# Queries of a half spaced apart, gathered rows in an old score tile, and four raw weight buffers, in a fused attention and mixture-of-experts kernel

## The chip, the cores and the metric

The kernel runs on one core of one Trainium2 chip. The metric is the device time of one execution in microseconds. Four engines do the work beside the DMAs: TensorE (PE, with its weight loads PEld), VectorE (DVE), ScalarE (ACT) and GpSimd (POOL); SyncE (SP) issues most DMAs.

## The reference

```python
# q, k, v: [8, 12, 448, 64]; w_pre, w_post: [12, 12]
scores = (1 / 8) * np.matmul(q, k.transpose(0, 1, 3, 2))
scores = np.einsum('bhij,hg->bgij', scores, w_pre)      # mixed over heads
attn = np.exp(scores - scores.max(-1, keepdims=True))
attn = attn / (attn.sum(-1, keepdims=True) + 1e-09)
attn = np.einsum('bhij,hg->bgij', attn, w_post)         # mixed again
x = np.matmul(attn, v).transpose(0, 2, 1, 3).reshape(3584, 768)

logits = x @ w_gate                                     # 8 experts, the best one each
expert_idx = np.argmax(logits, axis=1)
gate_w = softmax(logits)[arange, expert_idx]
for e in range(8):
    xe = x[expert_idx == e]
    out[expert_idx == e] = gate_w[...] * (np.maximum(xe @ w1[e], 0) @ w2[e])
# w1: [8, 768, 1024]; w2: [8, 1024, 768]; all float32
```

## The kernel before

**Attention.** A batch has four tiles of queries: three of 120 and one of 88, 32 tiles `T` in all. A tile is worked in blocks `s` of 20 queries (`NB`), a block in two halves `c` of 10 (`IB`); `geom` holds for each tile its batch, its number of queries and the sizes of the halves by block. A tile of 120 has six blocks, one of 88 five, the last with one half of 8. The steps of a tile:

- `qk` (L191 to L205): the scores of 6 pairs of heads, three matmuls per head (high and low parts of float32), copied from PSUM into the score tile `si` by ACT (L204) and DVE (L205). In `si` a partition is a query and holds 12 heads × 448 keys.
- `relayout` (L211 to L217): for each half one DMA on SP (L216) from `si` to `sb`, so that a partition of `sb` is a pair of query and head, 120 of them behind the first four. The four `sb` tiles are used in turn.
- `mix` (L219): one matmul per half with the 124 × 124 matrix `Wpre` (L226), which mixes the heads of each of ten queries; DVE takes the row maxima (L227), ACT the exponentials and their sums (L228).
- `weigh` (L233): reciprocals on DVE, and on POOL the second mixing matrix scaled by them, `wp` (L241).
- `post` (L245): four matmuls per half (L252), whose result is the mixed attention with the keys on partitions, then a copy of each half from PSUM into `PT` (L258), half 0 by ACT, half 1 by DVE. `PT` holds for each chunk of keys and each head the queries of the tile in order.
- `av` (L262): attention times `v` for the whole tile; `rows` (L278): its transposition, the store of the rows to DRAM (`XD`, L292) and the logits; `choose` (L298) and `dispatch` (L319): the expert of each query, its place in the expert's list, and a scatter of row number and gate weight into the table `TB`.

**The order of attention** is written out by hand (loop at L476). Step `u` of the loop issues the relayout of block u+2, the mix of u, the post of u−2, the weights of u, and then what is entered in `after` for that block: at the third block of a tile `values` (av) of the tile before and `scores` of the tile after, which makes that block long on PE (a burst); `rows` at the fourth and fifth; the load of the queries of T+2 (two DMAs on SP, L104) one block before the last; loads and splits of keys and values of the next batch. The last six steps load w1 of expert 0 (`load_w`): `fill_w` fetches 128 rows of raw weights on SP into a tile of the pool `wrp` (`raw`, L404), ACT casts the high part (L405), DVE subtracts for the low part (L406).

**The experts** (loop at L593) have a capacity of 512 rows each; further rows would be handled in a loop at the end. The first 256 rows of expert 0 are gathered and turned (transposed) while attention ends, into the old score tile of pool `si_p[0]` (`first_gather`, `first_turn`). For the rest `load_x` (L516) reads the expert's list (L518), makes row numbers of it on DVE (`ti` L521, `tcl` L522) and gathers the rows by indirect DMAs on POOL (L525) into `xs`; `turn_x` transposes them (L541); `hidden` computes relu(x·w1) (L558) and fills w2 on the way; `result` computes the output (L578), weighs it and scatters it (L587). The last slot of 128 rows of an expert is computed only when it has more than 384 rows. The order of instructions of this part is set by the framework's scheduler, which takes buffers as constraints.

Of the kernel before, what the change touches and what calls it, by code (L numbers as in the profile page):

```python
# [8 lines left out]
F32 = mybir.dt.float32  # L9
F32R = mybir.dt.float32r  # L10
# [26 lines left out]
ROWS = NE * NT  # L37
# [5 lines left out]
def attn_moe_kernel(ctx, tc, qT, kT, v, w_pre, w_post, w_gate, w1, w2, out):  # L43
    nc = tc.nc
# [4 lines left out]
    XD = dram.tile([NT, HD], F32, name="XD")  # L49
    TB = dram.tile([ROWS, 2], F32, name="TB")  # L50

    geom = []
    for T in range(NTILE):
        it = T % 4
        ni = min(IT, S - it * IT)
        geom.append((T // 4, it, ni, [[min(IB, ni - i) for i in range(s, min(s + NB, ni), IB)]
                                      for s in range(0, ni, NB)]))


    kq = ctx.enter_context(ExitStack())  # L60
# [1 line left out]
    q_p = kq.enter_context(tc.tile_pool(name="qp", bufs=1, side="right"))  # L62
# [5 lines left out]
    si_p.append(att.enter_context(tc.tile_pool(name="sip1", bufs=1)))  # L68
    sb_p = att.enter_context(tc.tile_pool(name="sbp", bufs=1))
    e_p = att.enter_context(tc.tile_pool(name="ep", bufs=4))  # L70
    sm_p = att.enter_context(tc.tile_pool(name="smp", bufs=4))
    pt_p = att.enter_context(tc.tile_pool(name="ptp", bufs=2))
    x_p = att.enter_context(tc.tile_pool(name="xp", bufs=1))
    ps_s = att.enter_context(tc.tile_pool(name="ps_s", bufs=1, space=PSUM))
# [22 lines left out]
        KK[b, c] = (kh, kl)  # L97

    def load_q(T):
        b, it, ni, _ = geom[T]  # L100
        qr = q_p.tile([P, NPAIR, IT], F32, name="qr")
        src = qT[b, :, H * it * IT:H * (it * IT + ni)].rearrange("d (c t i) -> t d c i", c=NPAIR, t=2)
        for half in range(2):
            nc.sync.dma_start(out=qr[half * D:(half + 1) * D, :, :ni], in_=src[half])  # L104
        QR[T] = qr
# [74 lines left out]
                   allow_small_or_imprecise_dtypes=True)  # L180


    none = sm_p.tile([P, ROWS // P // 8, 2], F32, name="none", bufs=1)
    nc.gpsimd.memset(none, 0.0)
    nc.gpsimd.iota(none[:, :, 0].bitcast(I32), pattern=[[0, ROWS // P // 8]], base=NOROW,
                   channel_multiplier=0)
# [2 lines left out]


    def qk(T, c):  # L191
        b, it, ni, _ = geom[T]
        if c == 0:
            SI[T] = si_p[T % 2].tile([IT, H, S], F32, name="si")
        kh, kl = KK[b, c]
        qh, ql = QQ[T]

        bs = bank_s[c % 2]
        for n, (qx, kx) in enumerate(((qh, kh), (qh, kl), (ql, kh))):
            for r in range(2):  # L200
                hs = slice(r * D, (r + 1) * D)
                nc.tensor.matmul(out=bs[:ni, r, :S], lhsT=qx[hs, c, :ni], rhs=kx[hs, :],  # L202
                                 start=(n == 0), stop=(n == 2))
        nc.scalar.copy(out=SI[T][:ni, 2 * c, :], in_=bs[:ni, 0, :S])  # L204
        nc.vector.tensor_copy(out=SI[T][:ni, 2 * c + 1, :], in_=bs[:ni, 1, :S])  # L205
# [5 lines left out]
    def relayout(T, s):  # L211
        sb = sbs[nsb["n"] % len(sbs)]
        nsb["n"] += 1
        for c, nq in enumerate(geom[T][3][s]):
            q0 = s * NB + c * IB
            nc.sync.dma_start(out=sb[R0:R0 + nq * H, c, :], in_=SI[T][q0:q0 + nq])  # L216
# [28 lines left out]
    def post(T, s):  # L245
        if s == 0:
            PT[T] = pt_p.tile([JC, NJ, H, IT], F32, name="pt")
        et, wp = EE.pop((T, s))
        for n, nq in enumerate(geom[T][3][s]):
            pp = bank_p[n]  # L250
            for c in range(NJ):
                nc.tensor.matmul(out=pp[:, c * IT:(c + 1) * IT],  # L252
                                 lhsT=et[:R1, n, c * JC:(c + 1) * JC],
                                 rhs=wp[:R1, n, :], start=True, stop=True)
        for n, nq in enumerate(geom[T][3][s]):
            i0 = s * NB + n * IB
            copy = (nc.scalar.copy, nc.vector.tensor_copy)[n]
            copy(out=PT[T][:, :, :, i0:i0 + nq].rearrange("p c h i -> p (c h) i"),  # L258
                 in_=bank_p[n][:, :NJ * IT].rearrange("p (x i) -> p x i", i=IB)[:, :, :nq])


    def av(T, g):  # L262
        b, it, ni, _ = geom[T]
        if g == 0:
            XT[T] = x_p.tile([P, NPAIR, IT], F32, name="xt")
        pa = bank_s[g][:, 0, :3 * IT].rearrange("p (c i) -> p c i", i=IT)
        for p in range(3):
            for c in range(NJ):
                for r in range(2):
                    h = 2 * (3 * g + p) + r  # L270
                    nc.tensor.matmul(out=pa[r * D:(r + 1) * D, p, :ni],  # L271
                                     lhsT=VV[b][:, c, h * D:(h + 1) * D],
                                     rhs=PT[T][:, c, h, :ni], start=(c == 0), stop=(c == NJ - 1))
        nc.vector.tensor_copy(out=XT[T][:, 3 * g:3 * g + 3, :ni], in_=pa[:, :, :ni])
# [201 lines left out]
    for u in range(NU + PLAG):  # L476
        if u + RLEAD < NU:
            relayout(*blocks[u + RLEAD])
        if u < NU:
            mix(*blocks[u])  # L480
        if u >= PLAG:
            post(*blocks[u - PLAG])
        if u < NU:
            weigh(*blocks[u])
            for what in after.get(blocks[u], []):
                what[0](*what[1:])
            T, s = blocks[u]
# [28 lines left out]
    def load_x(e, s0=0):  # L516
# [3 lines left out]
        tc_ = xs_p.tile([P, NS], I32, name="tcl", bufs=3)  # L520
        nc.vector.tensor_copy(out=ti, in_=tb[:, :, 0].bitcast(I32))  # L521
        nc.vector.tensor_scalar(out=tc_, in0=ti, scalar1=NT - 1, scalar2=None, op0=ALU.min)  # L522
        xs = xs_p.tile([P, NS, HD], F32, name="xs")
        for s in range(s0, NS):
            nc.gpsimd.indirect_dma_start(  # L525
                out=xs[:, s, :], out_offset=None, in_=XD[:, :],
                in_offset=bass.IndirectOffsetOnAxis(ap=tc_[:, s:s + 1], axis=0),
                bounds_check=NT - 1, oob_is_err=False)
        XS[e] = (xs, tb, ti)

    def turn_x(e, sl):
        xs = XS[e][0]
        if e not in XX:
            XX[e] = (xt_p.tile([P, NK1, CAP], F32R, name="xh"),
                     xt_p.tile([P, NK1, CAP], F32R, name="xl"))
        for half in range(2):
# [1 line left out]
            xh, xl = (t[:, ks, sl * P:(sl + 1) * P] for t in XX[e])  # L538
            px = pm_x.tile([P, 512], F32, name="pm_x")[:, :3 * P].rearrange("p (k x) -> p k x", x=P)
            for k in range(3):  # L540
                nc.tensor.transpose(out=px[:, k, :], in_=xs[:, sl, (3 * half + k) * P:  # L541
                                                            (3 * half + k + 1) * P], identity=ident)
            nc.scalar.copy(out=xh, in_=px)  # L543
            nc.vector.tensor_sub(out=xl, in0=px, in1=xh.bitcast(F32))
# [220 lines left out]
```

## Time and profile before

| what | value |
|---|---|
| time before, median of 3 runs | 1835.14 us (1822.03 to 1836.98) |
| the profiled execution's own time | 1846.31 us |
| its span | 1844.5 us, 30106 instructions |
| mean granted TensorE clock | 0.948 |
| DMA | 197.55 MB, mean 107 GB/s |
| attention | about 40 to 1205 us |
| experts | about 1230 to 1845 us |

The profile is of one execution. Engines are named PE, PEld, DVE, ACT and POOL; a `q` behind a name is the queue that issues (SPq). A group is written `line engine operation out<-in xcount`. Where an instruction starts late, the bracket behind it gives the idle time of its engine ahead of it and what ended that time. The granted clock is the share of full speed that TensorE was allowed to run at.

### The profile page before, as it was taken

What the parts mean: (1) busy time and instruction counts of PE and PEld (TensorE: products, weight loads), DVE (VectorE), ACT (ScalarE), POOL (GpSimd) and SP (SyncE); (2) the same over time, 40 slices, a digit from 0 to 9 for tenths busy, and PEclk for the clock granted to TensorE, in tenths of its full rate; (3) what the DMA queues carried; (4) which work ended last, traced back from release to release, by engine and by line L of the source; (5) the groups of instructions that cost most, each with busy time, mean ns of one, the idle gap of its engine ahead of it and who ended that gap; (6) DMA issues with size and microseconds to landing.
All of it is one profiled execution on the core that took longest, in us unless ns stands there. A gap on an engine that the chain in (4) does not pass through costs nothing. (4 is left out here: it accounts for less than half of the span.)

```text
span 1844.5 us, 30106 instructions
## 1 busy us (share of the span) xinstructions
PE 1572.8 (85%) x11200; PEld 1263.9 (69%) x11200; DVE 812.0 (44%) x2023; ACT 705.1 (38%) x1616; POOL 428.0 (23%) x595
## 2 busy tenths in 40 slices
PE   3798898788888798888789789769999898998996
PEld 1566566566566566666566567569887887897986
DVE  1455455555455455455455545541433324333330
ACT  2344445444444345344445444431423223223230
POOL 4223223223224124223322322210110101101000
PEclk9999899999999899899899989976999999999998
DMA  3554554454455355345455444541523325244230
GB/s 91 124 110 88 103 132 81 105 132 91 86 130 116 73 125 121 79 111 123 80 123 107 89 90 91 124 127 43 171 100 128 127 79 173 97 136 151 86 109 32
DMA packets 114741, 197.55 MB, mean 107 GB/s; under 512 B 40018, under 2 KB 89186, under 8 KB 114580
## 3 DMA queue, kind: packets, MB, share of 16 engines
q1 hardware_dynamic: 107472, 171.51, 39.2%
q0 software_dynamic: 6064, 23.86, 3.4%
q8 instruction: 101, 1.65, 0.4%
q14 instruction: 60, 0.49, 0.1%
q10 hardware_dynamic: 1044, 0.04, 0.0%
HBM read 96.02 MB, written 23.06 MB: 65 GB/s over the span
## 5 line engine op out<-in xcount | busy, mean ns | idle before, releaser
L226 PE MATMUL bm<-sb,Wpre 124*124 124x448 f32 x720 | 349.4, 594 | 151.8 <-DMA sb<-si 120.7
L252 PEld LDWEIGHTS bp<-wp,et 124*112 124x112 f32 x2880 | 346.0, 188 | 84.0 <-issue 81.9
L241 POOL TENSOR_SCALAR wp<-Wpost,st 124x120 f32<-124x120 f32 x360 | 206.2, 584 | 828.6 <-DVE st L238 725.8
L228 ACT ACTIVATE et<-bm,st 124x448 f32<-124x448 f32 x360 | 226.5, 632 | 328.9 <-DVE st L227 328.9
L252 PE MATMUL bp<-wp,et 124*112 124x120 f32 x2880 | 347.9, 277 | 5.0 <-ACT pt L258 5.0
L226 PEld LDWEIGHTS bm<-sb,Wpre 124*124 124x124 f32 x720 | 120.8, 196 | 267.0 <-issue 135.0
L227 DVE TENSOR_REDUCE st<-bm 124x1 f32<-124x448 f32 x360 | 218.3, 620 | 174.1 <-PE bm L226 163.4
L204 ACT COPY si<-bs 120x448 f32<-120x448 f32 (+1 forms) x192 | 102.1, 532 | 254.8 <-PE bs L202 248.1
L258 DVE COPY pt<-bp 112x480 f32<-112x480 f32 x176 | 115.6, 657 | 155.2 <-PE bp L252 139.2
L558 PE MATMUL pm_h<-xh,al 128*128 128x512 f32 (+2 forms) x384 | 153.7, 400 | 13.3 <-DVE al L406 13.3
L205 DVE COPY si<-bs 120x448 f32<-120x448 f32 (+1 forms) x192 | 119.3, 624 | 102.4 <-ACT si L204 91.5
L271 PE MATMUL bs<-pt,vt 112*64 112x120 f32 (+1 forms) x3072 | 157.7, 264 | 0.6 <-ACT pt L258 0.6
L558 PE MATMUL pm_h<-xh,ah 128*128 128x512 f32 (+2 forms) x384 | 152.3, 397 | 5.3 <-DVE hl L562 3.0
L271 PEld LDWEIGHTS bs<-pt,vt 112*64 112x64 f32 x3072 | 150.9, 140 | 4.7 <-ACT pt L258 0.9
L558 PE MATMUL pm_h<-xl,ah 128*128 128x512 f32 (+2 forms) x384 | 152.1, 396 | 0.0
L587 POOL DMA_INDIRECT out<-y,ti x30 | 34.3, 1142 | 499.1 <-ACT xh L543 327.4
L202 PE MATMUL bs<-kh,qh 64*120 64x448 f32 (+1 forms) x384 | 86.9, 449 | 50.3 <-DVE si L205 37.5
L578 PE MATMUL pm_y<-bh,hh 128*128 128x384 f32 x480 | 129.6, 348 | 0.0
L578 PE MATMUL pm_y<-bl,hh 128*128 128x384 f32 x480 | 128.5, 340 | 0.0
L578 PE MATMUL pm_y<-bh,hl 128*128 128x384 f32 x480 | 124.6, 340 | 0.0
L258 ACT COPY pt<-bp 112x480 f32<-112x480 f32 (+1 forms) x184 | 103.1, 560 | 5.9 <-PE bp L252 5.6
L202 PEld LDWEIGHTS bs<-kh,qh 64*120 64x120 f32 (+1 forms) x384 | 33.7, 172 | 101.0 <-DVE si L205 72.4
(115 smaller groups left out, 1914.3 us busy)
## 6 DMA issues: line engine op xcount, KB each, us to landing
sb<-si SPq DMA_DIRECT2D x352, 210.0 KB
wraw<-in_w SPq DMA_DIRECT2D x48, 512.0 KB
wraw<-in_w SPq DMA_DIRECT2D x64, 384.0 KB
kr<-in_kT SPq DMA_DIRECT2D x48, 224.0 KB
vt<-in_v SPq DMA_DIRECT2D x8, 1344.0 KB
qr<-in_qT SPq DMA_DIRECT2D x48, 180.0 KB
XD<-xr SPq DMA_DIRECT2D x24, 360.0 KB
qr<-in_qT SPq DMA_DIRECT2D x16, 132.0 KB
```

The source lines that it names most:

```text
L202: nc.tensor.matmul(out=bs[:ni, r, :S], lhsT=qx[hs, c, :ni], rhs=kx[hs, :], start=(n == 0), stop=(n == 2))
L204: nc.scalar.copy(out=SI[T][:ni, 2 * c, :], in_=bs[:ni, 0, :S])
L205: nc.vector.tensor_copy(out=SI[T][:ni, 2 * c + 1, :], in_=bs[:ni, 1, :S])
L226: nc.tensor.matmul(out=bm, lhsT=Wpre[:R1, :], rhs=sb[:R1, c, :], start=True, stop=True)
L227: nc.vector.reduce_max(out=st[:R1, 0, c:c + 1], in_=bm, axis=AX.X, negate=True)
L228: nc.scalar.activation(out=et[:R1, c, :], in_=bm, func=AF.Exp, bias=st[:R1, 0, c:c + 1], scale=1.0, accum_out=st[:R1, 1, c:c + 1])
L241: nc.gpsimd.tensor_scalar(out=wp[:R1, c, :], in0=Wpost[:R1], scalar1=st[:R1, 2, c:c + 1], scalar2=None, op0=ALU.mult)
L252: nc.tensor.matmul(out=pp[:, c * IT:(c + 1) * IT], lhsT=et[:R1, n, c * JC:(c + 1) * JC], rhs=wp[:R1, n, :], start=True, stop=True)
L258: copy(out=PT[T][:, :, :, i0:i0 + nq].rearrange("p c h i -> p (c h) i"), in_=bank_p[n][:, :NJ * IT].rearrange("p (x i) -> p x i", i=IB)[:, ...
L271: nc.tensor.matmul(out=pa[r * D:(r + 1) * D, p, :ni], lhsT=VV[b][:, c, h * D:(h + 1) * D], rhs=PT[T][:, c, h, :ni], start=(c == 0), stop=( ...
L558: nc.tensor.matmul(out=ph[:, :n], lhsT=wx[:, fs], rhs=xx[:, kt, xc], start=(m == 0), stop=(m == 3 * NK1 - 1))
L578: nc.tensor.matmul(out=py[g][:, :384], lhsT=hx[:, kt, ts], rhs=wx[:, g * 384:(g + 1) * 384], start=(n == 0), stop=(n == 3 * NK2 - 1))
```

## The change

Three things change.

- **The queries of a half.** A tile of `ni` queries has N = ceil(ni / 10) halves, 12 for 120 and 9 for 88. Half n now takes the queries n, n+N, n+2N and so on, where it took ten neighbours. `relayout` reads these partitions of `si`, and `post` writes its columns of `PT` with that step. In a tile of 88 the halves now hold 10 queries (seven of them) or 9 (two), where they held eight times 10 and once 8.
- **The gathered rows.** The pool tile `xs` is gone. The third and fourth slot of expert 0 go where its first two had been gathered, and the rows of all later experts go to the start of the old score tile, where expert 0's first turned rows had lain. This frees 12,288 bytes of each partition.
- **Buffers.** The raw weight pool gets four buffers instead of two, the pool of small tiles three instead of four; the constant tile `none` moves to the pool of the queries.

```diff
     for T in range(NTILE):
         it = T % 4
         ni = min(IT, S - it * IT)
-        geom.append((T // 4, it, ni, [[min(IB, ni - i) for i in range(s, min(s + NB, ni), IB)]
-                                      for s in range(0, ni, NB)]))
+        N = -(-ni // IB)
+        halves = [-(-(ni - n) // N) for n in range(N)]
+        geom.append((T // 4, it, ni, [halves[n:n + 2] for n in range(0, N, 2)], N))
+
+    def queries(T, s, c):
+        N, n = geom[T][4], 2 * s + c
+        return slice(n, n + N * (geom[T][3][s][c] - 1) + 1, N)
...
-    sm_p = att.enter_context(tc.tile_pool(name="smp", bufs=4))
+    sm_p = att.enter_context(tc.tile_pool(name="smp", bufs=3))
...
-    none = sm_p.tile([P, ROWS // P // 8, 2], F32, name="none", bufs=1)
+    none = q_p.tile([P, ROWS // P // 8, 2], F32, name="none")
...
         for c, nq in enumerate(geom[T][3][s]):
-            q0 = s * NB + c * IB
-            nc.sync.dma_start(out=sb[R0:R0 + nq * H, c, :], in_=SI[T][q0:q0 + nq])
+            nc.sync.dma_start(out=sb[R0:R0 + nq * H, c, :], in_=SI[T][queries(T, s, c)])
...
         for n, nq in enumerate(geom[T][3][s]):
-            i0 = s * NB + n * IB
             copy = (nc.scalar.copy, nc.vector.tensor_copy)[n]
-            copy(out=PT[T][:, :, :, i0:i0 + nq].rearrange("p c h i -> p (c h) i"),
+            copy(out=PT[T][:, :, :, queries(T, s, n)].rearrange("p c h i -> p (c h) i"),
                  in_=bank_p[n][:, :NJ * IT].rearrange("p (x i) -> p x i", i=IB)[:, :, :nq])
...
-                wpool["raw"] = moe.enter_context(tc.tile_pool(name="wrp", bufs=2, side="right"))
+                wpool["raw"] = moe.enter_context(tc.tile_pool(name="wrp", bufs=4, side="right"))
...
-        xs = xs_p.tile([P, NS, HD], F32, name="xs")
+
+        if s0:
+            xs = first_x["xs"]
+        else:
+            xs = si_p[0].tile([P, H, S], F32R, name="si").rearrange("p h j -> p (h j)")
+            xs = xs[:, :NS * HD].rearrange("p (s f) -> p s f", f=HD).bitcast(F32)
         for s in range(s0, NS):
             nc.gpsimd.indirect_dma_start(
-                out=xs[:, s, :], out_offset=None, in_=XD[:, :],
+                out=xs[:, s - s0, :], out_offset=None, in_=XD[:, :],
...
-                nc.tensor.transpose(out=px[:, k, :], in_=xs[:, sl, (3 * half + k) * P:
+                nc.tensor.transpose(out=px[:, k, :], in_=xs[:, sl - s0, (3 * half + k) * P:
```

The order of attention is that of before. Two places move. The first is the issue queue of SP in the last blocks of attention, where the first loads of w1 (`wraw`) stand between the last relayouts (`sb`). The square brackets list the semaphores that an instruction waits for: those of DMA queues (DMAHW), of DVE, PE and ACT. Before:

```order
L404 DMA wraw<-in_w 128x1024 [waits DMAHW0_49]
L216 DMA sb_147<-si 120x1x448 [waits DMAHW1_49,PE_49]
L216 DMA sb_147<-si 120x1x448 [waits DMAHW2_49,PE_49]
L404 DMA wraw<-in_w 128x1024 [waits DMAHW4_49,DMAHW3_49,DVE_49]
L216 DMA sb_148<-si 96x1x448 [waits PE_49]
L404 DMA wraw<-in_w 128x1024 [waits DMAHW5_49,DMAHW0_49,DVE_49]
L404 DMA wraw<-in_w 128x1024 [waits DMAHW6_49,DMAHW3_49,DVE_49]
L292 DMA XD<-xr 120x768 [waits DMAHW7_49,Activation_49]
```

After:

```order
L410 DMA wraw<-in_w 128x1024 [waits DMAHW0_49]
L223 DMA sb_147<-si 120x1x448 [waits DMAHW1_49,PE_49]
L223 DMA sb_147<-si 108x1x448 [waits DMAHW2_49,PE_49]
L410 DMA wraw<-in_w 128x1024 [waits DMAHW3_49]
L223 DMA sb_148<-si 108x1x448 [waits DMAHW4_49,PE_49]
L410 DMA wraw<-in_w 128x1024 [waits DMAHW5_49]
L410 DMA wraw<-in_w 128x1024 [waits DMAHW6_49,DVE_49]
L298 DMA XD<-xr 120x768 [waits DMAHW7_49,Activation_49]
```

Two of these loads lose their wait for DVE, and the last halves of the tile of 88 hold 9 queries (108 rows) instead of 10 and 8.

The second place is DVE at the end of an expert, where the last low parts of the next expert's w1 (`al`) are made, the third and the conditional fourth output (`y`) weighed, and the next list's row numbers (`ti`, `tcl`) taken from the loaded list `tb`. L645, or L656 of the change, is the branch around the fourth slot. Before:

```order
L406 TENSOR_TENSOR al_13032<-wraw,ah_13031 128x1024
L645 COMPARE_AND_BRANCH
L583 TENSOR_SCALAR y<-pm_y,tb 128x384
L645 UNCONDITIONAL_BRANCH x2
L406 TENSOR_TENSOR al_13106<-wraw,ah_13105 128x1024
L521 COPY ti<-tb 128x4
L406 TENSOR_TENSOR al_13112<-wraw,ah_13111 128x1024
L522 TENSOR_SCALAR tcl<-ti 128x4
L610 TENSOR_LOAD count
```

After:

```order
L412 TENSOR_TENSOR al_13025<-wraw,ah_13024 128x1024
L412 TENSOR_TENSOR al_13031<-wraw,ah_13030 128x1024
L412 TENSOR_TENSOR al_13105<-wraw,ah_13104 128x1024
L594 TENSOR_SCALAR y<-pm_y,tb 128x384
L412 TENSOR_TENSOR al_13111<-wraw,ah_13110 128x1024
L656 COMPARE_AND_BRANCH
L594 TENSOR_SCALAR y<-pm_y,tb 128x384
L656 UNCONDITIONAL_BRANCH x2
L621 TENSOR_LOAD count
```

The last two low parts stand ahead of the branch, and the copies of the row numbers have gone from here; they stand behind the next hidden layer's last rows now, ahead of its results.

More of the change, by code (lines that the diff above doesn't have):

```diff
@@ L99, in load_q @@
     def load_q(T):
-        b, it, ni, _ = geom[T]
+        b, it, ni = geom[T][:3]
         qr = q_p.tile([P, NPAIR, IT], F32, name="qr")
@@ L191, in qk @@
     def qk(T, c):
-        b, it, ni, _ = geom[T]
+        b, it, ni = geom[T][:3]
         if c == 0:
@@ L255, in post @@
         for n, nq in enumerate(geom[T][3][s]):
-            i0 = s * NB + n * IB
             copy = (nc.scalar.copy, nc.vector.tensor_copy)[n]
-            copy(out=PT[T][:, :, :, i0:i0 + nq].rearrange("p c h i -> p (c h) i"),
+            copy(out=PT[T][:, :, :, queries(T, s, n)].rearrange("p c h i -> p (c h) i"),
                  in_=bank_p[n][:, :NJ * IT].rearrange("p (x i) -> p x i", i=IB)[:, :, :nq])
     def av(T, g):
-        b, it, ni, _ = geom[T]
+        b, it, ni = geom[T][:3]
         if g == 0:
@@ L278, in rows @@
     def rows(T, part):
-        b, it, ni, _ = geom[T]
+        b, it, ni = geom[T][:3]
         if part == 0:
@@ L298, in choose @@
     def choose(T):
-        b, it, ni, _ = geom[T]
+        b, it, ni = geom[T][:3]
         lg2 = LG.pop(T)
@@ L319, in dispatch @@
     def dispatch(T):
-        b, it, ni, _ = geom[T]
+        b, it, ni = geom[T][:3]
         sc, ohb = LG.pop(T)
@@ L432, in attn_moe_kernel @@
     for T in range(NTILE):
-        b, it, ni, _ = geom[T]
+        b, it, ni = geom[T][:3]
         n = len(geom[T][3])
@@ L522, in load_x @@
         nc.vector.tensor_scalar(out=tc_, in0=ti, scalar1=NT - 1, scalar2=None, op0=ALU.min)
-        xs = xs_p.tile([P, NS, HD], F32, name="xs")
+        if s0:
[3 more added lines that the diff above has]
+            xs = xs[:, :NS * HD].rearrange("p (s f) -> p s f", f=HD).bitcast(F32)
         for s in range(s0, NS):
             nc.gpsimd.indirect_dma_start(
-                out=xs[:, s, :], out_offset=None, in_=XD[:, :],
+                out=xs[:, s - s0, :], out_offset=None, in_=XD[:, :],
                 in_offset=bass.IndirectOffsetOnAxis(ap=tc_[:, s:s + 1], axis=0),
                 bounds_check=NT - 1, oob_is_err=False)
-        XS[e] = (xs, tb, ti)
+        XS[e] = (xs, tb, ti, s0)
     def turn_x(e, sl):
-        xs = XS[e][0]
+        xs, s0 = XS[e][0], XS[e][3]
         if e not in XX:
@@ L568, in result @@
     def result(e, s):
-        tb, ti = first_x["rows"] if e == 0 and s < NE0 else XS[e][1:]
+        tb, ti = first_x["rows"] if e == 0 and s < NE0 else XS[e][1:3]
         hh, hl = HH[e]
```

## The prediction

> **What bounds the kernel now.** I read the header of the page first, then the waits, then busy time by stretch, and last single rows of the order of time.
>
> ```profile
> span 1844.5 us, 30106 instructions
> PE 1572.8 (85%) x11200; PEld 1263.9 (69%) x11200; DVE 812.0 (44%) x2023; ACT 705.1 (38%) x1616; POOL 428.0 (23%) x595
> ```
>
> PE is busy for 85% of the span, no other engine for half. So the time is PE's work, the time in which PE waits, and what PE loses when it runs at a lower clock. The rows of the waits in which PE is the one that waits (us in total, times, longest):
>
> ```profile
> PE bm L226 <- DMA sb<-si: 120.7, 90, 7.6
> PE bs L202 <- DVE si L205: 37.5, 62, 0.7
> PE bm L226 <- ACT et L228: 27.7, 22, 8.7
> PE pm_x L541 <- DMA xs<-XD,tcl: 14.2, 6, 3.0
> PE pm_h L558 <- DVE al L406: 13.3, 5, 3.8
> ```
>
> The largest by far is the mix matmul waiting for the relayout's DMA. Busy time by stretch (us: PE, PEld, DVE, ACT, POOL with their counts, then granted PE clock, DMA share, GB/s) tells what the stages are; the third stretch holds almost nothing but relayouts on the DMA engines, the fourth nothing but weight loads:
>
> ```profile
> 40.00:1205.00 1165.00, 980.76 (x8125) 732.12 (x8123) 598.42 (x1682) 521.71 (x1323) 339.24 (x496) 0.96 0.49 106
> 1230.00:1845.00 615.00, 565.35 (x2916) 514.73 (x2916) 199.01 (x297) 167.83 (x264) 71.28 (x61) 0.94 0.33 112
> 626.00:638.00 12.00, 9.83 (x101) 7.26 (x101) 2.91 (x8) 3.19 (x9) 3.20 (x5) 0.64 0.53 105
> 1700.00:1705.00 5.00, 4.76 (x20) 3.87 (x21) 2.70 (x4) 2.46 (x4) 0.00 (x0) 1.00 0.49 161
> ```
>
> Attention is 1165 us with 184 us of idle PE; the experts are 615 us with 50. A half that is relaid out holds 10 × 12 × 448 × 4 = 215,040 bytes. At the 105 GB/s of the third stretch that is 2.05 us, so 4.1 us for a block of two halves. What PE does for a plain block stands in its order of time:
>
> ```profile
> 644.56 1.77 PE L226 MATMUL bm<-sb,Wpre 124*124 124x448 f32 x4
> 646.16 1.80 PE L252 MATMUL bp<-wp,et 124*112 124x120 f32 x16
> 655.80 1.77 PE L226 MATMUL bm<-sb,Wpre 124*124 124x448 f32 x4
> 657.40 1.80 PE L252 MATMUL bp<-wp,et 124*112 124x120 f32 x16
> 660.04 0.99 PE L226 MATMUL bm<-sb,Wpre 124*124 124x448 f32 x2 [0.83 <-DMA sb<-si]
> 662.54 0.99 PE L226 MATMUL bm<-sb,Wpre 124*124 124x448 f32 x2 [1.51 <-DMA sb<-si]
> 627.60 1.82 PE L226 MATMUL bm<-sb,Wpre 124*124 124x448 f32 x2 [1.11 <-DMA sb<-si]
> ```
>
> A plain block starts its post 1.60 us after its mix and, by the row of 655.80, could start the next mix some 1.64 us after that: 3.2 us. The transfers need 4.1. Whenever plain blocks follow each other, as from 657.40 on, PE runs out of relaid scores. Burst blocks, which hold extra matmuls, let the DMAs catch up again. The last row shows the second loss: after such waits two mixes take 1.82 instead of 0.99 us, and the granted clock of that stretch is 0.64.
>
> **A. The relayout.** Bytes, counts and issues stay as they are; only the source partitions change, from ten neighbours to ten that lie 12 (or 9) apart. In the third stretch 0.53 of 16 engines, 8.5, move 105 GB/s, 12.4 GB/s each; in the fourth 0.49, 7.8 engines, move 161, 20.5 each. An engine that reads ten neighbouring partitions of SBUF is therefore served at 0.6 of the rate of one that spreads a load over 128. If the neighbourhood is the reason, 8.5 engines at 20.5 GB/s make 174 GB/s: 1.24 us for a half, 2.5 us for a block, less than PE's 3.2. If the read itself is slow, nothing changes (2.05 us). I take 1.24. [...]
>
> What remains is a queue. SP issues everything in order:
>
> ```profile
> 608.16 1.64 SPq L216 DMA_DIRECT2D sb<-si  x2
> 609.90 5.59 SPq L104 DMA_DIRECT2D qr<-in_qT  x2
> 615.58 1.72 SPq L216 DMA_DIRECT2D sb<-si  x2
> 617.39 2.58 SPq L292 DMA_DIRECT2D XD<-xr  x1
> 620.08 27.44 SPq L216 DMA_DIRECT2D sb<-si  x10
> ```
>
> Two issues of a relayout take 1.64 us, which a block of 3.2 hides. The two query loads hold SP for 5.59 us between two relayouts, once per tile; where a tile's first blocks are plain (8 batches) I leave 1.2 us each, 10 us in all. So of the 120.7 us of waiting 10 stay: **−111**.
>
> **B. The clock.** The granted clock of attention is 0.96. If it was low because PE stood still, as the rows from 627.60 suggest, 0.04 × 980.76 = 39 us come back with the waits; I take 36, since some waits stay: **−36**. Bounds: 0 and −39.
>
> **C. The copies into PT.** Each of the 360 copies now writes 480 values that lie 48 bytes (36 in a short tile) apart, where runs of ten lay together. What they cost now, and what their neighbours on the engines cost:
>
> ```profile
> L258 ACT COPY pt<-bp x184: 469/564/572, 56.7 to 1211.6; 112x480 f32<-112x480 f32 x176, 112x384 f32<-112x384 f32 x8
> L258 DVE COPY pt<-bp x176: 640/658/659, 58.1 to 1210.3; 112x480 f32<-112x480 f32 x176
> L228 ACT ACTIVATE et<-bm,st 124x448 f32<-124x448 f32 x360 | 226.5, 632 | 328.9 <-DVE st L227 328.9
> L227 DVE TENSOR_REDUCE st<-bm 124x1 f32<-124x448 f32 x360 | 218.3, 620 | 174.1 <-PE bm L226 163.4
> L204 ACT COPY si<-bs 120x448 f32<-120x448 f32 (+1 forms) x192 | 102.1, 532 | 254.8 <-PE bs L202 248.1
> L205 DVE COPY si<-bs 120x448 f32<-120x448 f32 (+1 forms) x192 | 119.3, 624 | 102.4 <-ACT si L204 91.5
> ```
>
> 448 contiguous values take 624 ns on DVE and 480 take 658: 34 ns for 32 values, about 1 ns each, and the same on ACT (532 to 564). No row shows a write with a step, so the bounds are nothing and, by twice the time per value, about 0.5 us a copy. A plain block has on DVE two maxima and a copy, 2 × 0.62 + 0.66 = 1.9 us, and some 0.3 for small ones; with 0.5 more it is 2.7 of the 3.2 that PE takes. ACT has 2 × 0.63 + 0.56 = 1.8, then 2.3. So plain blocks hide it, unless it stands in the chain from mix to weights; blocks with scores have two more copies of 0.53 and 0.62 and may not. If all 176 pairs showed their 0.5: +88. I take a tenth of that, rounded up: **+10**. [...]
>
> **D. The passage to the experts.** Four raw buffers instead of two: the second and third w1 loads no longer wait for a split on SP, in front of the relayouts.
>
> ```profile
> 1164.84 2.65 SPq L404 DMA_DIRECT2D wraw<-in_w  x1
> 1173.86 1.04 ACT L405 CAST ah<-wraw 128x1024 fp32r<-128x1024 f32 x1 [7.38 <-DMA wraw<-in_w]
> 1177.57 3.31 PE L226 MATMUL bm<-sb,Wpre 124*124 124x448 f32 x4 [8.71 <-ACT et L228]
> ```
>
> The longest wait, 8.71 us, is of this kind: ACT stood 7.38 us at the first split, whose load took 9.0 from issue to use, among relayouts; mix's exp stood behind it. The first load is still issued there, but among faster relayouts: I let 4 of 8.71 stay, about −5, and −4 for the two waits at SP. Against that, four more w2 splits (0.95 us on DVE each, row of 1553.09 below) come ahead of the last tile's choice, which the first expert's matmuls wait for: at worst +4, of which I take 3. Sum **−6**, bounds +4 and −20 (most of the 27.7 us).
>
> **E. An expert's start.**
>
> ```profile
> 1546.77 0.38 SPq L518 DMA_DIRECT2D tb<-TB  x1
> 1546.47 1.22 DVE L406 TENSOR_TENSOR al<-wraw,ah 128x1024 fp32r<-128x1024 f32 x1
> 1551.80 0.17 DVE L521 COPY ti<-tb 128x4 int32<-128x4 int32 x1 [4.12 <-DMA out<-y,ti]
> 1551.88 1.22 DVE L406 TENSOR_TENSOR al<-wraw,ah 128x1024 fp32r<-128x1024 f32 x1
> 1553.09 0.95 DVE L406 TENSOR_TENSOR bl<-wraw,bh 128x768 fp32r<-128x768 f32 x1
> 1553.16 0.79 PE L558 MATMUL pm_h<-xh,al 128*128 128x512 f32 x1 [3.12 <-DVE al L406]
> ```
>
> DVE stands 4.12 us at `ti`, whose rows SP asked for at 1546.77; the last split of w1 is queued behind it, and PE waits 3.12 for that split. In the new order both last splits stand ahead of that copy, which comes only behind the next hidden layer, still ahead of its gathers. That takes away the 13.3 us of the waits, and in proportion the clock: the experts lose 0.06 × 565 = 34 us by 50 us of idle PE, so 13.3 us cost up to 9, of which I take 5. Sum **−18**, bounds 0 and −22.
>
> **At nothing:** the gathered rows in the old score tile. A gather must wait until the last rows there have been turned, but PE turns the next expert's rows only after that anyway; `pm_x` keeps its 14.2 us. Its cover is the matmuls of the expert before; without it a gather's whole time, which the longest wait bounds below at 3.0 us, would show up to seven times. Three small-tile buffers instead of four: the next writer follows three blocks later, behind a post that PE has done by then.
>
> **The sum:** −111 − 36 + 10 − 6 − 18 = −161 us against the profiled execution, which took 1846.3 in all (the span of 1844.5 and 1.8 around it). The median of the runs shown is 1835.1, 11 lower; from there 1835.1 − 161 = 1674, rounded to **1673**.
>
> **Rivals.** (1) The copies pay doubly and everywhere: C is +88 instead of +10, so 1673 + 78 = 1751. For it: DVE and ACT stand in the chain of every block. Against it: both idle for half of attention (598 and 522 of 1165 us). (2) SBUF-to-SBUF reads are slow whatever their partitions: A and B fall away, 1835 + 10 − 6 − 18 = 1821. For it: every relayout in the trace has the same form, so no row separates the two. The low rate with so many engines busy speaks for a shared limit instead. (3) Another wait follows: SP's 5.59 us of query loads, or the `si` copies (37.5 us now) that scores and relayouts both wait for, give back half of A and B: 1673 + 74 = 1747. Against it: issues need 1.64 us a block. (4) Slower: the strided write makes DVE the bound. DVE has 598 us in attention; PE would need 1165 − 147 = 1018. From (1018 − 598)/176 = 2.4 us more per copy DVE decides, and from (1165 − 598)/176 = 3.2 it is worse than before. At 4 us more, seven times a copy's present time, attention is 598 + 704 = 1302 us, +137, with D and E 1835 + 137 − 24 = 1948. For it: no row bounds the write. Against it: seven times is far from any row.
>
> **Chances:** the forecast 0.71, rivals 0.13, 0.08, 0.05 and 0.03 in their order. The forecast's own range is 1640 to 1705, by the bounds of B to E. With rivals 1 and 3 the range is 1635 to 1757; rivals 2 and 4 stay out. Faster by over 1% (18 us, about what this measurement tells from no change) are the forecast, rivals 1 and 3 and a quarter of 2: 0.91; the same, the rest of 2: 0.06; slower 0.03.
>
> **What would show it.** A is right if PE's wait for `sb` falls under 25 us and a stretch of relayouts alone moves over 150 GB/s; B, if the granted clock of attention reaches 0.98 or more; C, by the medians of `pt` on ACT and DVE (under 1.2 us) and by PE's waits for `wp`, `et` and `bp`; D, if no wait for `et` is over 5 us; E, if the `al` wait is gone. The forecast is wrong if `sb` waits stay above 60 us, or if DVE is busier than 70% of attention.

## The result and the profile after

The changed kernel takes 1648.49 us (median of 4 runs, 1643.62 to 1658.73) where the kernel before takes 1836.06 in the same comparison: a ratio of 0.9009, 95% interval 0.8935 to 0.9082. One of the four runs of the kernel before took 2540 us; the ratio leaves it out. The forecast was 1673. The profiled executions are 1643.62 against 1846.31 us, 203 us apart; the sum had 161.

The page's header of the changed kernel: PE is busy for 91% of a span that is 11% shorter, and DVE and ACT have more to do.

```profile
span 1641.9 us, 30107 instructions
PE 1499.8 (91%) x11200; PEld 1218.6 (74%) x11200; DVE 860.0 (52%) x2023; ACT 766.2 (47%) x1616; POOL 426.6 (26%) x595
```

The waits of PE in the changed kernel (in total, times, longest):

```profile
PE bs L210 <- DVE si L213: 37.4, 62, 0.7
PE bm L233 <- ACT et L235: 19.8, 16, 5.3
PE pm_x L552 <- DMA si<-XD,tcl: 15.4, 6, 4.3
PE bm L233 <- DMA sb<-si: 10.1, 2, 5.9
```

The wait for `sb` went from 120.7 us in 90 places to 10.1 in two, and the row of `al` (13.3 us) is gone. That for `et` went from 27.7 to 19.8 us; `bs` and `pm_x` stand about where they stood.

Busy time by stretch of the changed kernel: attention, the passage, the experts (PE, PEld, DVE, ACT, POOL, granted clock, DMA share, GB/s):

```profile
40.00:1038.00 998.00, 928.55 (x8119) 705.04 (x8120) 643.76 (x1675) 581.72 (x1318) 337.39 (x493) 0.99 0.40 122
1038.00:1063.00 25.00, 11.94 (x122) 10.90 (x120) 11.11 (x25) 9.85 (x15) 1.57 (x1) 0.65 0.52 171
1063.00:1642.00 579.00, 542.05 (x2918) 496.05 (x2918) 197.41 (x306) 163.19 (x263) 69.12 (x61) 0.97 0.34 116
```

Attention went from 1165 to 998 us: 115 us of PE's idle time and 52 us of its busy time, for the same matmuls. The passage kept its 25 us or so (the edges are set by eye). The experts went from 615 to 579: 13 us idle, 23 busy.

The order of time on PE in attention, at two plain blocks after each other:

```profile
595.23 1.77 PE L233 MATMUL bm<-sb,Wpre 124*124 124x448 f32 x4
596.85 1.86 PE L259 MATMUL bp<-wp,et 124*112 124x120 f32 x16
598.76 1.77 PE L233 MATMUL bm<-sb,Wpre 124*124 124x448 f32 x4
600.37 1.86 PE L259 MATMUL bp<-wp,et 124*112 124x120 f32 x16
602.07 1.67 PE L233 MATMUL bm<-sb,Wpre 124*124 124x448 f32 x4
```

From mix to mix it is 3.53 and 3.31 us, no bracket stands behind any row, and no mix takes double time. The work of PE sets the step. A stretch with nearly nothing but relayouts on the DMA engines, 411 to 415 us, moves 231 GB/s, where before it was 105.

SP's query loads, before and after (duration of an issue, shortest, median, longest, in ns):

```profile
L104 SPq DMA_DIRECT2D qr<-in_qT x64: 616/2510/3319, 0.8 to 1124.2; - x64
```

```profile
L112 SPq DMA_DIRECT2D qr<-in_qT x64: 615/647/761, 0.8 to 961.5; - x64
```

The same issue that held SP for 2.5 us in the median takes 0.65 now. The long issues go with the neighbouring sources: the median is 2.51 and 2.45 us in the two experiments below that keep them (e2, e4), and 0.65 us in the two that space them (e1, e3). So the load itself is not slow; SP most likely stood there while relayouts ahead drained.

### The profile page after: what moved, and what is told of

It is laid out like the page before. It is cut to its first block, busy times and chain, and to the rows that moved or that the text cites. A ratio compares the mean times of both kernels' runs of the same rounds, so it can differ in the third digit from the quotient of the medians.

```text
span 1641.9 us, 30107 instructions
## 1 busy us (share of the span) xinstructions
PE 1499.8 (91%) x11200; PEld 1218.6 (74%) x11200; DVE 860.0 (52%) x2023; ACT 766.2 (47%) x1616; POOL 426.6 (26%) x595
## 5 line engine op out<-in xcount | busy, mean ns | idle before, releaser
L259 PEld LDWEIGHTS bp<-wp,et 124*112 124x112 f32 x2880 | 319.5, 178 | 85.9 <-issue 82.2
L233 PE MATMUL bm<-sb,Wpre 124*124 124x448 f32 x720 | 316.6, 562 | 33.7 <-ACT et L235 19.8
L259 PE MATMUL bp<-wp,et 124*112 124x120 f32 x2880 | 330.6, 268 | 5.3 <-ACT pt L264 5.3
L264 DVE COPY pt<-bp 112x480 f32<-112x480 f32 (+1 forms) x176 | 179.0, 1017 | 128.2 <-PE bp L259 120.5
L234 DVE TENSOR_REDUCE st<-bm 124x1 f32<-124x448 f32 x360 | 213.0, 618 | 17.7 <-PE bm L233 13.0
L264 ACT COPY pt<-bp 112x480 f32<-112x480 f32 (+1 forms) x184 | 186.4, 1013 | 2.1 <-PE bp L259 2.1
L569 PE MATMUL pm_h<-xh,ah 128*128 128x512 f32 (+2 forms) x384 | 143.7, 374 | 2.1 <-PEq L656 1.4
L569 PE MATMUL pm_h<-xl,ah 128*128 128x512 f32 (+2 forms) x384 | 144.6, 377 | 0.0
L569 PE MATMUL pm_h<-xh,al 128*128 128x512 f32 (+2 forms) x384 | 143.7, 374 | 0.0
L573 DVE SCALAR_TENSOR_TENSOR hl<-pm_h,hh 128x512 fp32r<-128x512 f32 (+3 forms) x72 | 43.3, 602 | 162.3 <-ACT hh L572 160.3
```

The costliest lines, as they stand in the source:

```text
L233: nc.tensor.matmul(out=bm, lhsT=Wpre[:R1, :], rhs=sb[:R1, c, :], start=True, stop=True)
L234: nc.vector.reduce_max(out=st[:R1, 0, c:c + 1], in_=bm, axis=AX.X, negate=True)
L259: nc.tensor.matmul(out=pp[:, c * IT:(c + 1) * IT], lhsT=et[:R1, n, c * JC:(c + 1) * JC], rhs=wp[:R1, n, :], start=True, stop=True)
L264: copy(out=PT[T][:, :, :, queries(T, s, n)].rearrange("p c h i -> p (c h) i"), in_=bank_p[n][:, :NJ * IT].rearrange("p (x i) -> p x i", i= ...
L569: nc.tensor.matmul(out=ph[:, :n], lhsT=wx[:, fs], rhs=xx[:, kt, xc], start=(m == 0), stop=(m == 3 * NK1 - 1))
```

## The experiments

**The two halves of the change, apart.** Four kernels make a square: sources spaced or neighbouring, and buffers or copies as before or as changed.

`e1_queries_only` puts the buffers back:

```diff
-    sm_p = att.enter_context(tc.tile_pool(name="smp", bufs=3))
+    sm_p = att.enter_context(tc.tile_pool(name="smp", bufs=4))
...
-                wpool["raw"] = moe.enter_context(tc.tile_pool(name="wrp", bufs=4, side="right"))
+                wpool["raw"] = moe.enter_context(tc.tile_pool(name="wrp", bufs=2, side="right"))
...
-        if s0:
-            xs = first_x["xs"]
-        else:
-            xs = si_p[0].tile([P, H, S], F32R, name="si").rearrange("p h j -> p (h j)")
-            xs = xs[:, :NS * HD].rearrange("p (s f) -> p s f", f=HD).bitcast(F32)
+        xs = xs_p.tile([P, NS, HD], F32, name="xs")
...
```

> The changed kernel with the buffers as they were (two raw weight buffers, gathered rows in a pool of their own, four small-tile buffers); only the queries of a half lie apart. Theory (spacing of the source partitions makes the relayouts fast, and that is all of attention's gain): PE's wait for sb under 20 us, attention as short as in the changed kernel, experts as long as before (615 us against 579), so about 1648 + 36 = 1685 us, 1675 to 1695. Rival (the buffers help attention too, or the spacing helps the experts): above 1710 or below 1665.

Measured: 1673.33 us (1665.5 to 1680.61), ratio to before 0.9073 (0.8993 to 0.9154). That is just under the range expected and in neither rival's; two executions took 1680 us and two 1666, which the clock explains below.

`e2_buffers_only` keeps neighbouring queries:

```diff
-        N = -(-ni // IB)
-        halves = [-(-(ni - n) // N) for n in range(N)]
+        halves = [min(IB, ni - i) for i in range(0, ni, IB)]
...
-        N, n = geom[T][4], 2 * s + c
-        return slice(n, n + N * (geom[T][3][s][c] - 1) + 1, N)
+        q0 = s * NB + c * IB
+        return slice(q0, q0 + geom[T][3][s][c])
```

> The changed kernel with ten neighbouring queries in a half, as before; only the buffers differ from before. Theory: PE's wait for sb stays at 110 to 130 us, the experts take 579 instead of 615 us, the time is about 1836 - 36 = 1800 us, 1785 to 1810. Rival (the weight buffers also unblock the relayouts, or the experts' gain needs the faster relayouts): sb waits under 90 us and under 1770, or no gain at all, 1825 to 1840.

Measured: 1811.53 us (1803.82 to 1818.16), ratio 0.985 (0.977 to 0.993), 1.5 us above the range expected: a small gain.

`e3_copies_in_runs` spaces the sources but lets the copies write runs of ten, `e4_neighbours_stepped_copies` does the reverse. In both the rows of a tile come out in another order. Both add a slice of neighbouring columns, `near`:

```diff
+    def near(T, s, c):
+        q0 = sum(sum(x) for x in geom[T][3][:s]) + sum(geom[T][3][s][:c])
+        return slice(q0, q0 + geom[T][3][s][c])
...
-            copy(out=PT[T][:, :, :, queries(T, s, n)].rearrange("p c h i -> p (c h) i"),
+            copy(out=PT[T][:, :, :, near(T, s, n)].rearrange("p c h i -> p (c h) i"),
```

```diff
-            nc.sync.dma_start(out=sb[R0:R0 + nq * H, c, :], in_=SI[T][queries(T, s, c)])
+            nc.sync.dma_start(out=sb[R0:R0 + nq * H, c, :], in_=SI[T][near(T, s, c)])
```

> The changed kernel, but the copies into PT write runs of ten again, so that the queries of a tile come out in another order (rows change places within a tile, nothing is left out). Theory (copies with a step are hidden behind PE): copies fall from 1.01 to 0.56 us on ACT and 0.66 us on DVE, the time stays at 1640 to 1650 us. Rival (the step costs time on the path): 88 us at most if all of it was exposed, so 1560 to 1630.

> The changed kernel, but the relayout reads ten neighbouring partitions again, while the copies into PT keep their step (rows change places within a tile, nothing is left out). Theory (the source partitions decide): relayouts alone move about 105 GB/s again, sb waits back at 100 to 130 us, time 1795 to 1815 us as with the buffers alone. Rival A (the copies, not the sources, changed the transfers, by less traffic of ACT and DVE in SBUF): sb waits under 60 us and under 1720 us. Rival B (the stepped copies cost time of their own): over 1830 us.

Measured: e3 1645.5 us (1633.48 to 1654.18), e4 1815.12 us (1809.21 to 1817.76), the one in its range and the other at its edge. PE's wait for `sb` in e1, e2, e3 and e4, in this order:

```profile
PE bm L233 <- DMA sb<-si: 8.8, 2, 4.6
```

```profile
PE bm L232 <- DMA sb<-si: 111.3, 89, 8.8
```

```profile
PE bm L237 <- DMA sb<-si: 10.4, 2, 6.2
```

```profile
PE bm L237 <- DMA sb<-si: 116.5, 85, 6.9
```

Only the source partitions decide on this wait: spaced 9 to 10 us, neighbouring 111 to 117, whatever the buffers or the copies do. The spacing is worth 1811.53 − 1648.49 = 163 us with the new buffers and 1839.64 − 1673.33 = 166 with the old ones (before in that comparison 1839.64); the buffers 25 and 28.

The copies in the changed kernel, and in e3:

```profile
L264 ACT COPY pt<-bp x184: 919/1012/1055, 49.4 to 1045.6; 112x480 f32<-112x480 f32 x176, 112x432 f32<-112x432 f32 x8
L264 DVE COPY pt<-bp x176: 918/1018/1067, 50.1 to 1043.7; 112x480 f32<-112x480 f32 x168, 112x432 f32<-112x432 f32 x8
```

```profile
L268 ACT COPY pt<-bp x184: 557/564/573, 49.8 to 1037.9; 112x480 f32<-112x480 f32 x176, 112x432 f32<-112x432 f32 x8
L268 DVE COPY pt<-bp x176: 601/657/660, 50.4 to 1036.5; 112x480 f32<-112x480 f32 x168, 112x432 f32<-112x432 f32 x8
```

With the step a copy takes 0.45 us more on ACT and 0.36 on DVE. The last copy on ACT starts 7.7 us earlier without it (1037.9 against 1045.6), so about 7 us of 176 × 0.36 = 63 are exposed. The medians of e3 and the changed kernel, 3 us apart, don't show it yet. All profiles together agree, though: in the six with spaced sources and the step the last copy on ACT starts at 1044.4 to 1046.1 us, in the four without the step at 1037.9 to 1040.5.

**The suspected costs by themselves.** `e5_alone` leaves nearly all of the computation out. Its patterns:

```python
for q in (slice(n, n + 109, 12) for n in range(8)):        # also steps 1, 2, 4
    nc.sync.dma_start(out=sb_half, in_=si[q])              # ten partitions
for q in (slice(4 * n, 4 * n + 97, 32) for n in range(8)): # also steps 1, 8
    nc.sync.dma_start(out=sb_half, in_=si[q])              # four partitions
for step in (1, 2, 3, 4, 8, 12):                           # DVE, then ACT
    copy(out=pt[:, :, slice(n, n + 9 * step + 1, step)], in_=src)
for width in (128, 256):                                   # with seven pauses
    ...
```

> No attention and no experts (nearly all of the computation is left out): three suspected costs by themselves. First, groups of eight relayout transfers: ten source partitions 1, 2, 4 and 12 apart (210 KB each), then four partitions 1, 8 and 32 apart (84 KB each). Theory (neighbouring partitions share a limit): 1 apart about 2.05 us a transfer as in the kernel before, 12 apart no more than the 0.78 us that SP needs to issue one, 2 and 4 apart between. Rival (what counts is distance): 32 apart is as fast as 8 apart. [...] Second, copies of 480 values from PSUM with a step of 1, 2, 3, 4, 8 and 12 values. Theory (a price per value once neighbours are gone): 1.01 us from step 4 on and no more at 12; rival (the price grows with the step): still rising from 4 to 12. Third, TensorE: a stream of wide matmuls, a pause of about 0.5 to 3 us, then 300 matmuls of 128 columns or 150 of 256. Theory: after some pauses the granted clock falls to 0.5, and the 128-column stream stays at 0.5 to its end, as in the 30.7 us after expert 0's start in the kernel before, while the 256-column stream is back after 3.4 to 6.8 us. Rival (the width has nothing to do with it): both come back after 3.4 to 6.8 us, or neither falls.

The windows hold, in order, ten partitions 1, 2, 4 and 12 apart and four partitions 1, 8 and 32 apart (the last two columns are DMA share and GB/s). Their edges are rough: the last transfers of a pattern reach into the next window.

```profile
8.00:24.00 16.00, 0.00 (x0) 0.00 (x0) 4.08 (x6) 0.00 (x0) 0.00 (x0) 1.00 0.52 94
24.00:37.00 13.00, 0.00 (x0) 0.00 (x0) 2.83 (x5) 0.00 (x0) 0.00 (x0) 1.00 0.56 137
37.00:47.00 10.00, 0.00 (x0) 0.00 (x0) 3.08 (x4) 0.00 (x0) 0.00 (x0) 1.00 0.54 173
47.00:54.00 7.00, 0.00 (x0) 0.00 (x0) 3.22 (x4) 0.00 (x0) 0.00 (x0) 1.00 0.65 248
54.00:67.00 13.00, 0.00 (x0) 0.00 (x0) 3.37 (x5) 0.00 (x0) 0.00 (x0) 1.00 0.25 58
67.00:75.00 8.00, 0.00 (x0) 0.00 (x0) 3.07 (x4) 0.00 (x0) 0.00 (x0) 1.00 0.25 82
75.00:84.00 9.00, 0.00 (x0) 0.00 (x0) 3.69 (x5) 0.00 (x0) 0.00 (x0) 1.00 0.24 80
```

The rate rises with the spacing, 94, 137, 173, 248 GB/s. Sharper is the time from pair to pair: DVE clears a tile as soon as the two transfers that wrote it, a pair, have landed. For ten partitions a pair of halves takes 4.1, 2.9, 2.3 and 1.7 us in the mean, which is 105, 149, 187 and 254 GB/s, and 105 is the rate of the kernel before. At 12 apart two issues of 0.77 us nearly fill the 1.7 us, so SP's issues most likely limit that rate, and what the partitions alone would allow is not seen. At 4 apart the pairs differ among themselves:

```profile
39.84 0.81 DVE L36 MEMSET sb<- 128x896 f32 x1 [2.17 <-DMA sb<-si]
42.38 0.81 DVE L36 MEMSET sb<- 128x896 f32 x1 [1.74 <-DMA sb<-si]
45.69 0.81 DVE L36 MEMSET sb<- 128x896 f32 x1 [2.51 <-DMA sb<-si]
47.51 0.81 DVE L36 MEMSET sb<- 128x896 f32 x1 [1.02 <-DMA sb<-si]
49.06 0.81 DVE L36 MEMSET sb<- 128x896 f32 x1 [0.75 <-DMA sb<-si]
```

The first row ends the pattern before. Of the four pairs the first two read partitions 0 to 39 and take 2.5 and 3.3 us, the last two read 40 to 79 and take 1.8 and 1.6. With one and the same spacing it matters which partitions are read, so distance alone does not set the rate. What makes 0 to 39 slower is not shown.

For fours the picture is less clear: neighbours are slow again (58 GB/s), but 8 and 32 apart differ little in their windows (82 and 80). The rows of the pairs 8 apart (first three) and of 32 apart (last three):

```profile
74.07 0.81 DVE L36 MEMSET sb<- 128x896 f32 x1 [0.93 <-DMA sb<-si]
75.89 0.81 DVE L36 MEMSET sb<- 128x896 f32 x1 [1.01 <-DMA sb<-si]
77.55 0.81 DVE L36 MEMSET sb<- 128x896 f32 x1 [0.86 <-DMA sb<-si]
...
81.00 0.81 DVE L36 MEMSET sb<- 128x896 f32 x1 [1.02 <-DMA sb<-si]
83.53 0.81 DVE L36 MEMSET sb<- 128x896 f32 x1 [1.73 <-DMA sb<-si]
85.85 0.81 DVE L36 MEMSET sb<- 128x896 f32 x1 [1.51 <-DMA sb<-si]
```

A pair takes 1.7 to 1.8 us at 8 apart; at 32 apart the first two take 1.6 and 1.8 and the last two 2.5 and 2.3. So 32 apart is as fast as 8 apart in two pairs and slower in two, which by itself decides little. What speaks against distance alone are the pairs 4 apart above.

The copies, four at a time, on DVE with steps of 1, 2, 3, 4, 8 and 12 values:

```profile
87.28 2.73 DVE L76 COPY pt<-bp 112x480 f32<-112x480 f32 x4
...
92.52 2.35 DVE L76 COPY pt<-bp 112x480 f32<-112x480 f32 x4 [2.50 <-ACT pt L79]
...
97.14 2.79 DVE L76 COPY pt<-bp 112x480 f32<-112x480 f32 x4 [2.27 <-ACT pt L79]
...
102.80 3.58 DVE L76 COPY pt<-bp 112x480 f32<-112x480 f32 x4 [2.87 <-ACT pt L79]
...
110.09 3.58 DVE L76 COPY pt<-bp 112x480 f32<-112x480 f32 x4 [3.70 <-ACT pt L79]
...
117.37 3.47 DVE L76 COPY pt<-bp 112x480 f32<-112x480 f32 x4 [3.70 <-ACT pt L79]
```

On DVE the price comes at a step of 4 values, 16 bytes, some 0.2 us for each copy within a row of four, and does not grow beyond. A copy takes 0.9 us there, not the 1.01 expected from the kernel. At a step of 3 values no price shows on DVE (2.79 us for the four against 2.73).

TensorE's part is told under the clock, below.

**The clock after expert 0's start.** The experts gained 36 us where 18 were forecast. The granted clock (sixth figure) of before, of the changed kernel, and of a second profile of the changed kernel (`e11_changed_again`), in the 30 us after expert 0's rows were turned:

```profile
1255.00:1286.00 31.00, 31.00 (x145) 30.90 (x145) 2.33 (x8) 2.22 (x8) 2.02 (x3) 0.51 0.15 48
```

```profile
1090.00:1120.00 30.00, 30.00 (x228) 29.97 (x228) 6.46 (x13) 7.08 (x15) 4.88 (x5) 1.00 0.24 79
```

```profile
1091.00:1121.00 30.00, 30.00 (x139) 29.90 (x139) 2.33 (x8) 1.95 (x8) 2.02 (x2) 0.50 0.15 50
```

In two of the three PE works without a gap for 30 us at half clock, mostly on matmuls of 128 columns (before: on these up to 1281.4 us, then mostly on ones of 384, at full clock again from 1286.6). The same kernel does it in one execution and not in another. Ahead of them PE pauses twice, in the changed kernel for 0.88 and 0.70 us in both profiles; here are the rows of the one that kept its clock:

```profile
1088.07 1.01 PE L552 MATMUL pm_x<-ident,si 128*128 128x128 f32 x6 [0.88 <-DVE xl L555]
1089.78 0.30 PE L569 MATMUL pm_h<-xh,ah 128*128 128x128 f32 x1 [0.70 <-ACT xh L554]
```

In e5 a stream of such matmuls after a pause, and one of 256 columns (both windows end in the 512-column matmuls that follow, the first from 209, the second from 922 us on):

```profile
150.00:214.00 64.00, 64.00 (x290) 62.94 (x290) 0.00 (x0) 0.00 (x0) 0.00 (x0) 0.50 0.00 1
904.00:945.00 41.00, 41.00 (x242) 36.80 (x240) 0.00 (x0) 0.00 (x0) 0.00 (x0) 0.96 0.00 1
```

After each of seven pauses of 0.79 to 2.58 us the 128-column stream fell to half and stayed there to its end, 60 us or more; the 256-column stream fell for 3.4 us after the pauses of 2.02 us and more, and not after shorter ones. The stretches at half clock in attention of the kernel before have such lengths too, 3.4, 6.8, 10.2 and once 13.7 us. The clock of the 128-column streams always fell 2.2 to 3.7 us after the pause began, so e5 tried only part of the ways in which pause and clock can meet, and how often it happens is not read from it. A stream without a pause ahead was not run there.

`e6_turn_earlier` takes the pause away by other work:

```diff
-            hidden(0, EARLY, x=first_x["x"])
+            hidden(0, EARLY, x=first_x["x"], fts=range(NK2 - 2))
             for s in range(NE0, NS):
                 turn_x(0, s)
+            hidden(0, EARLY, x=first_x["x"], fts=range(NK2 - 2, NK2))
...
```

> The changed kernel, with the turning of expert 0's third and fourth slot put between the sixth and seventh of eight parts of its first hidden layer, so that PE no longer pauses ahead of the 128-column matmuls (0.88 and 0.70 us there). Theory (that pause, by chance of its phase, sets off 30.7 us at half clock in some executions, some 15 us): no execution over 1650 us, mean clock at least 0.976 in all, median 1640 to 1645. Rival (those executions are long for another reason): the spread of 1644 to 1659 us stays.

Measured: 1640.08 us (1636.31 to 1644.3 in 6 runs), mean clocks 0.977 to 0.983. Its clock in the 128-column stretch:

```profile
1085.00:1110.00 25.00, 25.00 (x209) 25.00 (x208) 4.06 (x12) 3.28 (x11) 4.03 (x4) 1.00 0.21 65
```

The long executions are gone, as the theory has it. Of all profiles, the eight of kernels with the pause hold the 30 us at half clock four times (before, e1, e10, e11), the five of kernels without it (e6 to e9, e12) never. `e9_queries_and_turn` does the same to e1 (the diff is that of e6):

> As e1_queries_only (buffers as before), with the earlier turning of e6_turn_earlier. Theory (of the buffers' 25 us a part is the chance of the 30.7 us at half clock, which needs PE's pause at expert 0's start): no such stretch, 1655 to 1662 us, so the buffers are worth 15 to 22 us against e6_turn_earlier's 1640. Rival (the stretch belongs to the two raw buffers): the stretch stays and with it 1670 us or more.

Measured: 1661.59 us (1659.86 to 1665.7), its clocks 0.976 to 0.98. So with the pause gone the buffers are worth 1661.59 − 1640.08 = 21.5 us, or 17 by the ratios to the kernel before that ran beside each (0.9018 and 0.8924), and the stretch does not belong to two raw buffers.

`e10_two_raw` undoes the number of raw buffers alone:

```diff
-                wpool["raw"] = moe.enter_context(tc.tile_pool(name="wrp", bufs=4, side="right"))
+                wpool["raw"] = moe.enter_context(tc.tile_pool(name="wrp", bufs=2, side="right"))
```

> The changed kernel with two raw weight buffers again; the gathered rows stay in the old score tile. Theory (the number of raw buffers alone makes the experts' gain, the place of the rows nothing): PE waits 13 to 14 us for al again, 1665 to 1682 us as e1_queries_only. Rival (the place of the rows is part of it): under 1660 us.

Measured: 1678.25 us (1671.64 to 1686.34), and the wait for `al` is back:

```profile
PE pm_h L569 <- DVE al L412: 14.7, 6, 4.0
```

The place of the gathered rows gives nothing itself; it makes room for the raw buffers.

**Versions beyond the change.** `e7_runs_and_turn` is e6 with the copies of e3, and the host lays the queries out so that spaced partitions hold neighbours:

```diff
+    def place(ni):
+        N = -(-ni // IB)
+        where = [p for n in range(N) for p in range(n, ni, N)]
+        return _np.argsort(where)
...
-            inputs["q"][:, :, i:i + IT].transpose(0, 3, 1, 2).reshape(B, D, -1)
+            inputs["q"][:, :, i + place(min(IT, S - i))].transpose(0, 3, 1, 2).reshape(B, D, -1)
```

> As e6_turn_earlier, and the queries of a tile are laid out on the host in such an order that spaced partitions hold neighbouring queries: the relayout reads spaced partitions, the copies into PT write runs of ten again, and the rows come out in order. Theory: the copies' 7 us of e3_copies_in_runs come on top of e6_turn_earlier, 1632 to 1640 us. Rival (they are noise): within 2 us of e6_turn_earlier.

Measured: 1632.89 us (1629.33 to 1638.11), 7.2 under e6. That is the copies' price again. `e8_slot3_later` moves the turning of the fourth slot (and the next list's load behind it):

```diff
-    def result(e, s):
+    def result(e, s, amid=lambda: None):
...
         for kt in range(NK2):
+            if kt == 5:
+                amid()
...
```

> As e7_runs_and_turn, and the turning of an expert's fourth slot is put behind five eighths of the third slot's result instead of ahead of it, since PE waits 15.4 us in six places for its gather. Theory: most of that wait and some of the clock behind it goes, 1612 to 1628 us. Rival (the wait moves: the fourth slot is late for the next hidden layer): no faster than e7_runs_and_turn.

Measured: 1644.97 us (1644.04 to 1649.06), 12 slower than e7. PE's waits for the rows and, new, for the weight split in front of their copy:

```profile
PE pm_x L556 <- DMA si<-XD,tcl: 14.9, 4, 4.5
PE pm_x L556 <- DVE al L416: 8.0, 2, 4.4
```

The wait for the rows did not shrink (12.8 us in six places in e7), it moved and took another with it; the rival was right. The last two runs compare the changed kernel and e7 on one chip:

> The changed kernel as it is, on the same chip as the version that follows, to compare the two: 1645 to 1652 us, with single executions up to 1660 in which the clock stays at half after expert 0's start.

> e7_runs_and_turn once more beside the changed kernel: 10 to 18 us under it, 1630 to 1640 us. Rival (the two differ by no more than the chips): less than 5 us apart.

Measured: 1652.08 us (1645.73 to 1662.86) and 1630.62 us (1628.72 to 1638.68); ratios to before 0.8959 (0.8913 to 0.9006) and 0.8848 (0.8811 to 0.8884). Of e11's six executions three took about 1646 us at a mean clock of 0.979 and three 1658 to 1663 at 0.969 to 0.971. e7 is 21 us under the changed kernel, more than the 10 to 18 expected; its executions all lie below the changed kernel's.

## Why the prediction was right, and where it was off

- **A, the relayout (−111): right.** 120.7 − 10.1 = 110.6 us are gone, by the sources alone (e1 to e4); why neighbouring partitions are read more slowly is not shown. Rival 2, that the read is slow whatever its partitions, is out (e5: 254 against 105 GB/s). A half takes about 0.9 us where the sum took 1.24, and both are hidden. Not right is what was to remain: the 10 us are two waits at the kernel's start, 4.2 and 5.9 us, where 16.4 us were before; behind the query loads nothing waits, since their 2.5 us per issue went too. The amount was met by chance.
- **B, the clock (−36): right.** Read in stretches of one microsecond, the granted clock of attention falls short of full speed by about 50 us in sum before and by 7 after; weighted with PE's busy share of each stretch, by 41 and 4. So 37 to 43 us came back, and they go with the waits: unweighted, the shortfall is 50 to 58 us in e2 and e4 and 7 to 9 in e1 and e3. PE's busy time fell by 52, past the bound of 39. All of the fall lies in `bm` (592 ns in the mean before, 557 after) and `bp` (277 and 268). The sum has no term for the 9 to 15 us of it that the clock does not explain, and their cause stays open.
- **C, the copies (+10): right.** About 7 us (e7 against e6 7.2, the last copy of e3 7.7 earlier). A copy costs 0.36 to 0.45 us more, under the 0.5 that doubling would have meant, and nine tenths are hidden.
- **D, the passage (−6): nearer to nothing.** The wait of 8.7 us for `et` became one of 5.3, just over the 5 named, and all waits for `et` in the last 66 us of attention went from 9.3 to 5.3. The last tile's choice made PE wait 3 us longer (`lg`, `sc` and `nbase` together 9.2, then 12.3), as the sum's +3 had it. The 4 us that two waits on SP were to give show in no wait of PE, and the stretch from attention to experts kept its 25 us.
- **E, the expert's start (−18): mechanism right, mis-sized.** The `al` wait went as forecast. The profiled experts gained 36, because the profile of before held a 30.7 us stretch at half clock, 15 us of loss, that has nothing to do with the stall of `al`; spreading the lost clock over all stalls in proportion hid it. Freed of that stretch the buffers give 17 to 21.5 us (e9 to e6), against 24 for D and E.

The sum against the profiled execution was 42 us short, of it 18 in E and 16 in PE's busy time in attention, where the clock itself explains at most 7 of the 16. Between the medians it was 1836.06 − 1648.49 = 188 against 161. The last step of the sum, 1674 rounded to 1673, is a slip of 1 us.

## What to carry to other kernels

When a DMA moves a few partitions of SBUF, look at GB/s in a stretch that holds nothing else, and at what the busy engines reach in another stretch. Here the relayouts moved 105 GB/s at a DMA share of 0.53 where weight loads moved 161 at 0.49; with the partitions spread, at the cost of an index, they moved 231 at 0.64. Put the scattered order where it is free, in the layout of an input, rather than in a write with a step: at 16 bytes and more a copy took 0.9 us in e5 instead of 0.7, and the kernel without the step was 7.2 us faster (e7 against e6). And before a stretch of lost clock is charged to the stalls, look where it lies in time: here one stretch of 30.7 us at half clock cost 15 us, more than the 13.3 us of the waits for `al`, and in the changed kernel such a stretch was there in one execution and not in another.

## What the runs showed of the hardware

- After pauses of PE ahead of a stream of 128-column matmuls (0.97 and 0.70 us in the kernel before, 0.88 and 0.70 in the changed one) the granted clock was at 0.5 for some 30 us in four of the eight profiles of kernels with these pauses, while PE was busy without a gap. In the kernel before it was 30.7 us, the last 5.2 of them mostly on matmuls of 384 columns. In e5 it fell to 0.5 after all seven pauses of 0.79 to 2.58 us and stayed there to the end of the 128-column stream, some 60 us; a stream of 256 columns fell only after pauses of 2.02 us and more, and was back after 3.4 us.
- An issue of the query loads on SP took 2.51 us in the median in the kernel before and 2.51 and 2.45 in e2 and e4, whose relayouts read neighbouring partitions, and 0.65 in the changed kernel, e1 and e3, whose relayouts read spaced ones. The load was the same in all.
- A DMA that reads ten partitions of SBUF and writes 120 moved 105 GB/s from neighbours and 149, 187 and 254 from partitions 2, 4 and 12 apart (e5); the last rate is close to what SP's issues of 0.77 us allow. At 4 apart a pair took 2.5 and 3.3 us from partitions 0 to 39, and 1.8 and 1.6 from 40 to 79.
